# A fused attention and gated-GELU kernel on one core: the first stage put in another order (x ahead on two queues, exponentials grouped, M early, w_out clamped on VectorE)

## The chip, the cores and the metric

The kernel runs on one core of one Trainium2 chip. The metric is the device time of one execution in microseconds (us), as the median of several executions. All runs told here are in the same, fast state, and all of them gave correct results.

In views of the profile, PE is TensorE (matrix products), PEld its weight loads, DVE is VectorE, ACT is ScalarE, POOL is GpSimd, and SP the engine that issues most transfers. `L383` is line 383 of that kernel's own source, so the numbers of one statement differ between kernels.

## The reference, cut to what matters

```python
def _attn_ref(x, state):                       # x (8, 8, 512, 64), state (8, 8, 32, 64), fp32
    scores = scale * np.matmul(x, state.transpose(0, 1, 3, 2))
    a = softmax(scores)                        # (written out with max, exp and sum)
    xread = np.matmul(a, state)                # 512 tokens of a batch read the state
    scores2 = scale * np.matmul(state, x.transpose(0, 1, 3, 2))
    a2 = softmax(scores2)
    sread = np.matmul(a2, x)                   # 32 states of a batch read x
    return np.concatenate([xread, sread], axis=2)

def _moe_ref(x, w_in, w_out):                  # x (4352, 512), w_in (512, 2048), w_out (2048, 512)
    h = x @ w_in
    g = h * (1.0 / (1.0 + np.exp(-1.702 * h)))
    return (g @ w_out).astype(np.float32)
```

The weights arrive as 64-bit floating point. The kernel reads each number as two 32-bit words and puts a 32-bit number together from them with integer operations, on VectorE for the most part.

## The kernel before

Four ideas are needed for the argument.

**M.** `xread @ w_in` is computed as `a @ (state @ w_in)`. `M(b, c)` is the state of batch b times chunk c (512 columns) of w_in. An `up` tile then is four products of M with the softmax `aT`, followed by a gelu on ScalarE; `down` is the product with w_out. Batch b has 16 `up` tiles, four for each chunk; I call four of them a turn.

**Pieces.** w_in has 16 pieces of 128 x 512 numbers (piece 4c + k belongs to chunk c), w_out has 16 too. Each has two parts. `round_a` takes the exponent field and clamps it; `round_b` makes the number. Before, the clamp is two Relus on ScalarE for pieces 0 to 7 and two operations on POOL for all others.

```python
    def round_a(i):
        _, hi = words(i)
        sc = wpool.tile([P, FC], I32, tag="sc", name=f"sc_{i}", bufs=3)
        power[i] = sc
        nc.vector.tensor_scalar(sc, hi, 0x7FF00000, None, ALU.bitwise_and)
        if i >= 2 * NPR:
            nc.gpsimd.tensor_scalar(sc, sc, most, least, ALU.min, ALU.max)
            nc.gpsimd.tensor_scalar(sc, sc, -least, 8.0, ALU.add, ALU.mult)
            return
        nc.scalar.activation(out=sc.bitcast(FP32), in_=sc, func=AF.Relu, bias=edge[0], scale=-8.0)
        nc.scalar.activation(out=sc, in_=sc.bitcast(FP32), func=AF.Relu, bias=edge[1], scale=-1.0)

    def round_b(i):
        # ... cut: dst is the piece's place in w_in or w_out
        nc.vector.tensor_scalar(fr, hi, 0xFFFFF, 0x100000, ALU.bitwise_and, ALU.bitwise_or)
        nc.vector.scalar_tensor_tensor(sc, hi, -0x80000000, sc, ALU.bitwise_and, ALU.bitwise_or)
        nc.vector.scalar_tensor_tensor(dst, lo, 2.0**-32, fr, ALU.mult, ALU.add)
        nc.vector.scalar_tensor_tensor(dst, dst, 2.0**-20, sc.bitcast(FP32), ALU.mult, ALU.mult)

    AHEAD = 2                                   # exponents taken ahead of the piece that is rounded
```

**State reads.** Softmax over the tokens (exponentials on ScalarE, normalisation on VectorE), four transposes `eT` for each half, then 32 small products `sr`.

**Order.** Every engine takes its instructions in the order in which the program issues them. So where a statement stands in the program decides what waits behind what. This is the first stage of the kernel before:

```python
    load_weights(1)                             # piece 0, half a MB, ahead of x
    load_state(0)
    load_x(0)                                   # four chunks, all on SP's queue
    load_weights(NPR)
    # ...
    keep_warm(8)                                # products of zeros that keep TensorE's clock up
    round_to(1, 0)                              # piece 0
    att_state(0)
    att_xT(0, 0, 3)                             # three warm-up products before each x chunk
    # ... cut: scores and softmax of batch 0, piece 1, the same for batch 1, pieces 2 and 3

    def chunk(b, c, beside=()):
        round_to(NPR * (c + 1))
        att_M(b, c)
        for i in range(nper):
            up_x(b, nper * c + i)
            if i < len(beside):
                beside[i]()
    # ...
    chunk(0, 0, [lambda: None, lambda: att_x_exp(1), x_norm_1])
    chunk(1, 0, [rounds(1), rounds(1), rounds(1)])
    chunk(0, 1, [lambda: powers_to(done["b"] + 2), lambda: s_softmax(0), rounds(1), rounds(1)])
    chunk(1, 1, [rounds(1), rounds(1)])
    s_read(0)
    chunk(0, 2, [lambda: powers_to(done["b"] + 2), lambda: s_softmax(1), rounds(1), rounds(1)])
    s_read(1)
    chunk(0, 3, [rounds(1), rounds(1), rounds(1)])

    rest = list(range(2 * nper, NF))
    for f in range(NF):                         # the f loop: down of batch 0, rest of up of batch 1
        round_to(NFC * NPR + f + 1)
        for r in range(SCH):
            down(0, r, [f], out_x[0, r], r == SCH - 1)
        if f % 2:
            if rest[0] % nper == 0:
                att_M(1, rest[0] // nper)
            up_x(1, rest.pop(0))
        pace(1.5)
    # ... cut: batches 1 to 7
```

## Time and profile before

| kernel before | |
|---|---|
| median of the first 3 runs | 876.31 us (875.25 to 876.94) |
| span of the profiled run, mean granted clock | 874.7 us, 0.985 |
| PE busy | 851.0 us (97%) |
| f loop | 116.3 to 189.1 us |
| PE idle between 28.5 and 189.1 us | 15.1 us |

The profile page draws the span as 40 slices with one digit each (tenths of busy time). The other views used below are stretches (busy time of each engine between two times), the waits of an engine, and one engine's instructions in order of time. In that order a line has its start, its length, the engine and line, the operation, its tiles, and in brackets how long the engine had stood still before it and what ended that. The prediction below shows the main lines of before. Five more, in PE's order of time, are needed to weigh the result. The first is where the work that is compared later begins; the other four are the 20 us ahead of the f loop:

```profile
28.51 1.08 PE L251 MATMUL M<-w_in,stT 64*32 64x512 f32 x12
...
92.97 5.92 PE L334 MATMUL sr<-eT,xn 128*128 128x64 f32 x32 [1.48 <-ACT eT L327]
98.81 4.39 PE L251 MATMUL M<-w_in,stT 64*32 64x512 f32 x12
104.83 1.92 PE L251 MATMUL M<-w_in,stT 64*32 64x512 f32 x4 [1.63 <-DVE w_in L183]
107.42 9.07 PE L375 MATMUL h<-aT,M 128*128 128x512 f32 x16 [0.67 <-ACT M L317]
```

The groups of the last four lines take elsewhere in this trace 3.79 (the state read at 76.22), 1.08 (twelve products of M at 52.16), 1.05 (the last four at 29.87) and 7.13 us (a turn at 82.45). So the loss of these 20 us is not in brackets alone: TensorE also works slowly, because its clock is halved after the waits and because M(0,3) gets its pieces one by one.

### The profile page before, as it was taken

The page shows a single profiled execution, that of the slowest core. Times are in us where ns is not written, and L with a number is a line of the kernel's source. Part 1 is how long each engine was busy: PE and PEld are TensorE (multiplying, and loading weights), DVE is VectorE, ACT ScalarE, POOL GpSimd, SP SyncE. Part 2 cuts the span into 40 slices and gives each one's busy share as a digit, 9 for nine tenths or more (in the row PEclk, how much of TensorE's full clock was granted, in tenths as well). Part 3 has the DMA queues.
Part 4 walks back from the last instruction along what each step waited for, and adds up shares of the span by engine and source line. Part 5 has one row for each costly group of instructions (what it writes and reads, how often), then busy time and mean ns, then how long its engine had stood idle before and what let it go on. Part 6 is the DMA issues. An engine that isn't in the chain of part 4 may idle for free.

```text
span 874.7 us, 6893 instructions
## 1 busy us (share of the span) xinstructions
PE 851.0 (97%) x2892; PEld 394.0 (45%) x2892; DVE 222.9 (25%) x370; ACT 199.9 (23%) x335; POOL 59.2 (7%) x90
## 2 busy tenths in 40 slices
PE   8889799999999999999999999999999999999997
PEld 3324444444354435444454435443544447744443
DVE  5856999203300050005000230005000500000000
ACT  4653310112123120412122212312041212103100
POOL 0012444010000000000000000000000000000000
PEclk9999699999999999999999999999999999999999
DMA  9602045310020001200030003000000000000000
GB/s 242 244 1 96 7 153 163 69 52 12 25 61 0 16 13 29 44 3 25 12 61 4 12 21 64 1 12 13 13 12 1 24 13 13 1 12 12 13 12 24
DMA packets 43134, 35.04 MB, mean 40 GB/s; under 512 B 36832, under 2 KB 36832, under 8 KB 43104
## 3 DMA queue, kind: packets, MB, share of 16 engines
q1 hardware_dynamic: 40000, 25.69, 10.8%
q0 software_dynamic: 3104, 8.92, 2.8%
q8 instruction: 22, 0.36, 0.2%
q14 instruction: 8, 0.07, 0.0%
HBM read 25.69 MB, written 8.91 MB: 40 GB/s over the span
## 4 chain that ended last, share of the span: by engine, by line
issue 71%; PE 19%; DVE 5%; ACT 2%; POOL 2%; DMA 1%; SPq 0%; POOLq 0%; DVEq 0%; ACTq 0%
PE o L400 11%; PE h L375 5%; POOL out_dram L408 2%; PE M L251 1%; DVE w_in L182 1%; DVE sc L181 1%; DVE w_in L183 1%; DMA xn<-in_x_dram 1%; ACT g L377 0%; ACT M L317 0%; PE sr L334 0%; PE xT L243 0%; DVE sc L165 0%; PE s L251 0%; DVE fr L180 0%
## 5 line engine op out<-in xcount | busy, mean ns | idle before, releaser
L400 PE MATMUL o<-w_out,g 128*128 128x512 f32 x1024 | 456.3, 595 | 0.0
L400 PEld LDWEIGHTS o<-w_out,g 128*128 128x128 f32 x1024 | 188.8, 190 | 232.3 <-issue 231.3
L375 PE MATMUL h<-aT,M 128*128 128x512 f32 x512 | 231.0, 607 | 9.5 <-ACT M L317 6.1
L375 PEld LDWEIGHTS h<-aT,M 128*128 128x128 f32 x512 | 98.0, 194 | 142.1 <-issue 115.0
L377 ACT ACTIVATE g<-h 128x512 f32<-128x512 f32 x128 | 76.1, 597 | 169.7 <-PE h L375 169.6
L317 DVE COPY M<-M 128x512 f32<-128x512 f32 x24 | 16.4, 682 | 194.6 <-PE M L251 194.6
L408 POOL DMA_DIRECT2D out_dram<-osb x32 | 17.5, 548 | 644.7 <-ACT osb L407 644.5
L407 ACT COPY osb<-o 128x512 f32<-128x512 f32 x32 | 18.7, 585 | 136.1 <-PE o L400 133.8
L251 PE MATMUL M<-w_in,stT 64*32 64x512 f32 x512 | 43.9, 615 | 2.7 <-DVE w_in L183 2.7
L317 ACT COPY M<-M 128x512 f32<-128x512 f32 x40 | 22.6, 587 | 83.9 <-PE M L251 83.9
L334 PEld LDWEIGHTS sr<-eT,xn 128*128 128x128 f32 x256 | 31.8, 203 | 5.6 <-issue 2.9
L334 PE MATMUL sr<-eT,xn 128*128 128x64 f32 x256 | 31.8, 286 | 2.3 <-ACT eT L327 2.3
L234 DVE COPY stT<-stT 128x128 f32<-128x128 f32 x6 | 1.7, 290 | 117.2 <-PE stT L232 117.2
L244 ACT COPY xT<-xT 128x512 f32<-128x512 f32 x18 | 10.3, 586 | 91.0 <-PE xT L243 91.0
L375 PE MATMUL h_sr<-srT,w_in 128*128 128x256 f32 x128 | 27.8, 379 | 0.0
L400 PE MATMUL o_sr<-w_out,g 128*128 128x512 f32 x64 | 27.6, 592 | 0.0
L244 DVE COPY xT<-xT 128x512 f32<-128x512 f32 x14 | 9.7, 692 | 65.5 <-PE xT L243 65.5
L375 PEld LDWEIGHTS h_sr<-srT,w_in 128*128 128x128 f32 x128 | 24.3, 190 | 3.7 <-issue 0.5
L167 POOL TENSOR_SCALAR sc<-sc 128x512 int32<-128x512 int32 x24 | 17.3, 722 | 110.4 <-DVE sc L165 110.4
L243 PEld LDWEIGHTS xT<-ident,xn 128*128 128x128 f32 x128 | 15.7, 141 | 16.9 <-issue 12.7
L264 DVE STREAM_TRANSPOSE e<-s 128x512 f32<-128x512 f32 x16 | 10.5, 694 | 47.1 <-PE s L251 47.1
L343 DVE COPY srT<-sr 64x128 f32<-64x128 f32 x6 | 1.7, 283 | 81.4 <-PE sr L334 81.4
(64 smaller groups left out, 393.1 us busy)
## 6 DMA issues: line engine op xcount, KB each, us to landing
xn<-in_x_dram SPq DMA_DIRECT2D x32, 256.0 KB
raw_o<-in_moe_w_out_dram SPq DMA_DIRECT2D x16, 512.0 KB
out_dram<-osb POOLq DMA_DIRECT2D x32, 256.0 KB, 2.3
w_out<-in_moe_w_in_dram SPq DMA_DIRECT2D x12, 512.0 KB
raw_i<-in_moe_w_in_dram SPq DMA_DIRECT2D x4, 512.0 KB
stn<-in_state_dram SPq DMA_DIRECT2D x16, 32.0 KB
out_dram<-osb_sr POOLq DMA_DIRECT2D x2, 256.0 KB, 7.1
```

The source lines that it names most:

```text
L167: nc.gpsimd.tensor_scalar(sc, sc, most, least, ALU.min, ALU.max)
L243: nc.tensor.transpose(ps[:, c], x_heads(b, c, j), ident)
L244: copies(b or None, j)(A[b]["xT"][:, j], ps.rearrange("p c q -> p (c q)"))
L251: nc.tensor.matmul(ps[g][st], A[b]["stT"][rows, st], rhs(rows, j), start=True, stop=True)
L264: nc.vector.transpose(t[:, g].rearrange("p i n -> p (i n)"), a["s"][g])
L317: copies(b, g)(m[:, g], ps[g])
L334: nc.tensor.matmul(ps[:, j], x_heads(b, c, j), a["eT"][:, :, c, Ns * j : Ns * (j + 1)], start=(c == 0), stop=(c == SCH - 1),)
L375: nc.tensor.matmul(hps, lhs[i], rhs[i], start=(i == 0), stop=(i == n - 1))
L377: nc.scalar.activation(out=gt[:, :ntok], in_=hps, func=AF.Gelu_apprx_sigmoid)
L400: nc.tensor.matmul(ops, G[key, f][:, P * r : P * (r + 1)], w_out[:, f], start=(f == 0), stop=(f == NF - 1))
L407: nc.scalar.copy(osb, ops)
L408: nc.gpsimd.dma_start(dst, osb)
```

## The change

Its intent is to close the holes of the first stage. x is to come before the weights, on two queues. The exponentials of both batches' state reads are to share one swap of ScalarE's function table instead of two. `M` is to be computed ahead of its turn where that is possible. The clamp of w_in goes wholly to ScalarE and that of w_out to VectorE, so that POOL no longer works beside VectorE. Exponents are taken three pieces ahead, but only within w_in. The state reads move into the f loop, spread out. (Left out of the diff: the fraction of a piece, `fr`, is made in place instead of in a tile of its own, and the function for the state reads' softmax is cut into maximum, exponential and normalisation.)

```diff
@@ load_x
-            nc.sync.dma_start(xn[b][:, c], x_v[b, c])
+            queue = nc.scalar if b == 0 and c % 2 else nc.sync
+            queue.dma_start(xn[b][:, c], x_v[b, c])
@@ round_a                                     (AHEAD is 3 now; sc has AHEAD + 1 buffers)
-        if i >= 2 * NPR:
-            nc.gpsimd.tensor_scalar(sc, sc, most, least, ALU.min, ALU.max)
-            nc.gpsimd.tensor_scalar(sc, sc, -least, 8.0, ALU.add, ALU.mult)
+        if PIECES[i][0] == "o":
+            nc.vector.tensor_scalar(sc, sc, most, least, ALU.min, ALU.max)
+            nc.vector.tensor_scalar(sc, sc, -least, 8.0, ALU.add, ALU.mult)
             return
@@ round_to
-            powers_to(done["b"] + 1 + ahead)
+            powers_to(min(done["b"] + 1 + ahead, max(NFC * NPR, done["b"] + 1)))
@@ the first stage (cut: two and 24 warm-up products instead of three and 18, order of the head)
-    load_weights(1)
     load_state(0)
     load_x(0)
...
-    round_to(1, 0)
     att_state(0)
-    att_xT(0, 0, 3)
+    att_xT(0, 0, 2)
...
+    att_blocks(1)
+    att_x_exp(1)
+    up_x(0, 0)
+    up_x(0, 1)
+    up_x(0, 2, True)                            # True: a PSUM tile of another pool
+    up_x(0, 3, True)
+    round_to(NPR + 1)
+    att_x_norm(1)
+    att_M(1, 0)
+    # turn(b, c, then, n): the four up of a turn, M of "then" before the last, n pieces beside
+    turn(1, 0, None, [1, 1])
+    round_to(2 * NPR)
+    att_M(0, 1)
+    turn(0, 1, (1, 1), [1, 1, 1])
+    turn(1, 1, None, [1])
+    round_to(3 * NPR)
+    att_M(0, 2)
+    att_s_max(0)
+    att_s_max(1)
+    turn(0, 2, None, [1, 1, 1])
+    room = apool.tile([P, NPR, S], FP32, tag="xT", name="e2_0")
+    att_s_exp(0, room)
+    att_s_exp(1)
+    round_to(4 * NPR)
+    att_M(0, 3)
+    att_s_norm(0)
+    att_s_norm(1)
+    turn(0, 3, None, [1, 1])
@@ the f loop
     for f in range(NF):
+        rounds(1)
         round_to(NFC * NPR + f + 1)
         for r in range(SCH):
             down(0, r, [f], out_x[0, r], r == SCH - 1)
-        if f % 2:
-            if rest[0] % nper == 0:
-                att_M(1, rest[0] // nper)
+        if f in (0, nper * 2):
+            att_M(1, 2 + f // (nper * 2))
+        if f in (0, 2):
+            for g in range(NG):
+                att_eT(f // 2, g)
+        if f in (1, 3):
+            att_sread(f // 2)
+        if f % 2 == 1:
             up_x(1, rest.pop(0))
-        pace(1.5)
```

More of the change, by code (lines that the diff above doesn't have):

```diff
@@ L127 @@
     raw, power = {}, {}
+    AHEAD = 3
     def load_weight(i):
@@ L162, in round_a @@
         _, hi = words(i)
-        sc = wpool.tile([P, FC], I32, tag="sc", name=f"sc_{i}", bufs=3)
+        sc = wpool.tile([P, FC], I32, tag="sc", name=f"sc_{i}", bufs=AHEAD + 1)
         power[i] = sc
         nc.vector.tensor_scalar(sc, hi, 0x7FF00000, None, ALU.bitwise_and)
-        if i >= 2 * NPR:
-            nc.gpsimd.tensor_scalar(sc, sc, most, least, ALU.min, ALU.max)
-            nc.gpsimd.tensor_scalar(sc, sc, -least, 8.0, ALU.add, ALU.mult)
+        if PIECES[i][0] == "o":
+            nc.vector.tensor_scalar(sc, sc, most, least, ALU.min, ALU.max)
+            nc.vector.tensor_scalar(sc, sc, -least, 8.0, ALU.add, ALU.mult)
             return
@@ L175, in round_b @@
         dst = w_in[key[1]][:, key[2]] if key[0] == "i" else w_out[:, key[1]]
+        fr = dst.bitcast(I32)
         lo, hi = words(i)
         sc = power.pop(i)
-        fr = wpool.tile([P, FC], I32, tag="fr", name=f"fr_{i}")
         nc.vector.tensor_scalar(fr, hi, 0xFFFFF, 0x100000, ALU.bitwise_and, ALU.bitwise_or)
@@ L184, in round_b @@
         del raw[i]
-    AHEAD = 2
     done = {"load": 0, "a": 0, "b": 0, "credit": 0.0}
@@ L264, in att_blocks, with att_s_max, att_s_exp @@
             nc.vector.transpose(t[:, g].rearrange("p i n -> p (i n)"), a["s"][g])
-    def att_s_exp(b):
+    def att_s_max(b):
+        a = A[b]
+        a["mx2"] = []
+        for g in range(NG):
+            mx = apool.tile([P, 1], FP32, tag="mx2", name=f"mx2_{b}_{g}", bufs=4)
+            nc.vector.tensor_reduce(out=mx, in_=a["s"][g], axis=AX.X, op=ALU.max, negate=True)
+            nc.vector.tensor_scalar(mx, mx, scale, None, ALU.mult)
+            a["mx2"].append(mx)
+    def att_s_exp(b, room=None):
         a = A[b]
@@ L269, in att_s_exp, with att_s_norm @@
         for g in range(NG):
-            mx = apool.tile([P, 1], FP32, tag="mx2", name=f"mx2_{b}_{g}", bufs=2)
-            nc.vector.tensor_reduce(out=mx, in_=a["s"][g], axis=AX.X, op=ALU.max, negate=True)
-            nc.vector.tensor_scalar(mx, mx, scale, None, ALU.mult)
-            e = apool.tile([P, S], FP32, tag="e2", name=f"e2_{b}_{g}", bufs=2)
-            sm = apool.tile([P, 1], FP32, tag="sm2", name=f"sm2_{b}_{g}", bufs=2)
-            nc.scalar.activation(out=e, in_=a["s"][g], func=AF.Exp, bias=mx, scale=scale, accum_out=sm)
+            e = apool.tile([P, S], FP32, tag="e2", name=f"e2_{b}_{g}", bufs=2) if room is None else room[:, g]
+            sm = apool.tile([P, 1], FP32, tag="sm2", name=f"sm2_{b}_{g}", bufs=4)
+            nc.scalar.activation(out=e, in_=a["s"][g], func=AF.Exp, bias=a["mx2"][g], scale=scale, accum_out=sm)
             a["e2"].append((e, sm))
-    def att_s_softmax(b):
+    def att_s_norm(b):
         for e, sm in A[b]["e2"]:
@@ L356, in att_slots @@
         at(5, att_blocks, b)
+        at(5, att_s_max, b)
         at(5, att_s_exp, b)
         at(5, att_x_exp, b)
-        at(5, att_s_softmax, b)
+        at(5, att_s_norm, b)
         at(5, att_x_norm, b)
@@ L369, with up @@
     G = {}
-    def up(key, f, ntok, lhs, rhs):
-        hps = psH.tile([P, ntok], FP32, tag="h", name=f"h_{key}_{f}")
+    def up(key, f, ntok, lhs, rhs, spare=False):
+        hps = att_ps([P, ntok], f"h_{key}_{f}") if spare else psH.tile([P, ntok], FP32, tag="h", name=f"h_{key}_{f}")
         n = len(lhs)
@@ L378, in up, with up_x @@
         G[key, f] = gt
-    def up_x(b, f):
+    def up_x(b, f, spare=False):
         c, o = divmod(P * f, FC)
         m = A[b]["M", c]
-        up(b, f, S, [m[:, g, o : o + P] for g in range(NG)], [A[b]["aT"][:, g] for g in range(NG)])
+        up(b, f, S, [m[:, g, o : o + P] for g in range(NG)], [A[b]["aT"][:, g] for g in range(NG)], spare)
     def up_s(f):
@@ L408, in down, with rounds @@
             nc.gpsimd.dma_start(dst, osb)
-    load_weights(1)
+    nper = FC // P
+    def rounds(n):
+        round_to(done["b"] + n)
     load_state(0)
@@ L425 @@
     att_scores(0)
-    powers_to(2)
+    powers_to(1)
     att_blocks(0)
     att_x_exp(0)
+    powers_to(2)
     round_to(2, 1)
     att_x_norm(0)
-    keep_warm(18)
+    keep_warm(24)
     att_state(1)
@@ L436, with turn @@
     att_scores(1)
-    keep_warm(18)
-    round_to(NPR, 1)
-    nper = FC // P
-    def chunk(b, c, beside=()):
-        round_to(NPR * (c + 1))
-        att_M(b, c)
+    keep_warm(24)
+    powers_to(4)
+    round_to(NPR, 2)
+    att_M(0, 0)
+    att_blocks(1)
[7 more added lines that the diff above has]
+    att_M(1, 0)
+    def turn(b, c, then, n=()):
         for i in range(nper):
+            if i == nper - 1 and then:
+                att_M(*then)
             up_x(b, nper * c + i)
-            if i < len(beside):
-                beside[i]()
-    powers_to(NPR + 1)
-    att_blocks(1)
-    def x_norm_1():
-        round_to(NPR + 1, 1)
-        att_x_norm(1)
-    def s_softmax(b):
-        att_s_exp(b)
-        att_s_softmax(b)
-    def s_read(b):
-        for g in range(NG):
-            att_eT(b, g)
-        att_sread(b)
-    def rounds(n):
-        return lambda: round_to(done["b"] + n)
-    chunk(0, 0, [lambda: None, lambda: att_x_exp(1), x_norm_1])
-    chunk(1, 0, [rounds(1), rounds(1), rounds(1)])
-    chunk(0, 1, [lambda: powers_to(done["b"] + 2), lambda: s_softmax(0), rounds(1), rounds(1)])
-    chunk(1, 1, [rounds(1), rounds(1)])
-    s_read(0)
-    chunk(0, 2, [lambda: powers_to(done["b"] + 2), lambda: s_softmax(1), rounds(1), rounds(1)])
-    s_read(1)
-    chunk(0, 3, [rounds(1), rounds(1), rounds(1)])
+            if i < len(n):
+                rounds(n[i])
+    turn(1, 0, None, [1, 1])
[16 more added lines that the diff above has]
+    turn(0, 3, None, [1, 1])
     rest = list(range(2 * nper, NF))
     for f in range(NF):
+        rounds(1)
         round_to(NFC * NPR + f + 1)
@@ L484 @@
             down(0, r, [f], out_x[0, r], r == SCH - 1)
-        if f % 2:
-            if rest[0] % nper == 0:
-                att_M(1, rest[0] // nper)
+        if f in (0, nper * 2):
+            att_M(1, 2 + f // (nper * 2))
+        if f in (0, 2):
+            for g in range(NG):
+                att_eT(f // 2, g)
+        if f in (1, 3):
+            att_sread(f // 2)
+        if f % 2 == 1:
             up_x(1, rest.pop(0))
-        pace(1.5)
     load_state(2)
```

## The prediction

> **What bounds the kernel now.** I read three views in this order: the 40 slices of the page, the busy time by stretch, and the chain of waits with the order of time of each engine.
>
> ```profile
> PE   8889799999999999999999999999999999999997
> DVE  5856999203300050005000230005000500000000
> PEclk9999699999999999999999999999999999999999
> ```
>
> TensorE (PE) is full from the seventh slice on; the loss is in the first six, where VectorE (DVE) is the busier of the helpers, and one slice has a low clock. The stretches put numbers on it:
>
> ```profile
> 28.50:116.30 87.80, 74.18 (x273) 32.99 (x273) 65.84 (x110) 39.87 (x66) 21.57 (x27) 0.86 0.20 72
> 116.30:189.10 72.80, 71.29 (x194) 30.62 (x193) 41.92 (x61) 8.69 (x15) 19.17 (x24) 1.00 0.39 108
> 189.10:874.70 685.60, 680.09 (x2295) 319.09 (x2293) 96.00 (x168) 138.63 (x234) 17.71 (x32) 1.00 0.07 19
> ```
>
> Columns: stretch, length, then busy time of PE, weight load, DVE, ACT, POOL, then granted clock. From 189.1 us (the `down` of batch 1) PE is busy 680 of 686 us, and the change touches nothing there. So the question is only when that point is reached. The useful PE work between 28.5 and 189.1 us at full clock is: 32 `up` tiles at 1.72 us (55.0), 64 `down` products at 0.859 (55.0), 8 `M` blocks at 1.05 (8.4), two eT at 0.88 (1.8), two state reads at 3.5 (7.0; both as the later batches show them): 127 us of 160.6. About 33 us are lost, nearly all before 116 us.
>
> The chain of waits shows how, in the third turn:
>
> ```profile
> 60.07 1.28 ACT L275
> 61.36 1.45 ACT e L275 x4
> 62.83 1.28 ACT L377
> 64.12 1.09 ACT g L377 x2
> 65.21 0.49 ACT M L317
> 65.74 8.85 PE h L375 x16
> ```
>
> ScalarE (ACT) swaps its function table for two exponentials and back, so the gelus and the copy of `M` queue up behind it and PE starts at 65.74 although `M` was ready at 63.87. The sum of the waits has the other side: DVE stood still for those exponentials, twice, while weight pieces were still to be rounded.
>
> ```profile
> DVE sm L281 <- ACT e L275: 16.1, 2, 9.4
> ```
>
> Those 16 us come back at 90 to 105 us, where PE waits for the last four pieces of w_in. Two more lines, from DVE's order of time, show what a piece costs alone and beside POOL:
>
> ```profile
> 27.81 0.69 DVE L181 SCALAR_TENSOR_TENSOR sc<-w_out,sc 128x512 int32<-128x512 int32 x1
> 64.42 1.10 DVE L181 SCALAR_TENSOR_TENSOR sc<-raw_i,sc 128x512 int32<-128x512 int32 x1
> ```
>
> From start to start a piece takes 2.60 us with POOL quiet (27.14 to 29.74) and 3.54 with POOL clamping (63.75 to 67.29). Last, the clock after an idle stretch of PE (39.75 to 42.83):
>
> ```profile
> 42.00:43.00 1.00, 0.17 (x1) 0.20 (x2) 1.00 (x3) 1.00 (x3) 0.00 (x0) 1.00 0.00 0
> 43.00:44.00 1.00, 1.00 (x2) 0.44 (x2) 1.00 (x3) 0.01 (x1) 0.00 (x0) 0.54 0.00 0
> 46.00:47.00 1.00, 1.00 (x3) 0.53 (x2) 0.39 (x2) 0.61 (x2) 0.77 (x2) 0.75 0.00 0
> ```
>
> It is halved for 3.4 us (43.05 to 46.5), which costs 1.7; again 3.4 us from 66.9, and 17 us from 94.3.
>
> **What the Trainium skill says.** (1) "TensorE: Matmul & The Clock Gate", section "What's actually happening": the clock is halved after an idle window of 3413 ns; the windows run free. The trace agrees: 43.05, 66.94, 94.3 and 111.3 lie on one grid of 3.413 us. Windows with about 45% of PE work or less were punished, one with about 60% was not (53.3 to 56.7). (2) "ScalarE: Activation LUTs", "What ACT_TABLE_LOAD costs": 1283 ns plus a drain of about 1380 for each switch. The load agrees (1.28); the drain doesn't show: the exponential starts at 61.36, 1.29 after the load began. I use 1.3 a switch. (3) "GPSIMD Engine Reference", "8. Key points": POOL shares its SBUF interfaces with DVE, with contention for instructions of two SBUF inputs. It agrees: 0.69 against 1.10 above. (4) "VectorE: DVE Perf Modes", "The perf-mode tier table": tensor_scalar in fp32 runs at 2x from SBUF. In this trace the int32 bit operation of a piece (0.34 from start to start) is about twice as fast as the two-input ones (0.60 to 0.70). Whether min/max and add/mult on int32 do so is not shown; I assume 0.37 each.
>
> **The change part by part.** I walk the four in-order queues of the changed build with the durations above (gelu 0.60, ACT's two Relus 1.37 a piece, copy of `M` to first `up` 0.64, result of a matmul 0.26 after its issue, exponential of 512 columns 0.72).
>
> x ahead: before, the four chunks of x land at 6.5, 7.7, 8.9, 9.95, behind 0.5 MB of weights. Without these, and issued from two queues, I take the last at 7.7 (an estimate: the same 1.2 us a chunk from 2.3, plus landing). The scores of batch 0 end at 11.75 instead of 13.94: 2.2 gained.
>
> The head of DVE: piece 0 was rounded in DVE's idle time while x came; now it comes after the scores. From 11.75: blocks, maximum, subtraction 3.75, then pieces 0 and 1 (2.60 each), norm 4.27, pieces 2 and 3 with two more exponents taken ahead (5.54): 30.5, against 29.87. So the 2.2 are spent and 0.6 more; the first `up` starts at 32.2 (31.59 before).
>
> Batch 1 exponentials ahead of the gelus: one table swap before the four `up` of batch 0, which spare PSUM lets run through (to 39.1). Then the trap: in ACT's order the exponents of pieces 6 and 7 (2 x 1.37) stand ahead of the copy of `M` (1,0). Last gelu 40.0, exponents to 42.75, `up` (1,0) at 43.4; before 42.83. PE idles 0.9 + 2.3 us here.
>
> w_in clamped on ACT instead of POOL for pieces 8 to 15: 0.94 us less on DVE for each, 7.5 in all, for 1.37 each on an ACT that is at 45%. Pieces 4 to 7 are ready at 49.3 (before 54.0), PE gets to `M` (0,1) at 50.3; its copy waits behind one exponent, `up` (0,4) at 53.1 (before 55.72). `M` (1,1) ahead of its turn: its copy runs under `up` (0,7), gap 0.55 instead of 1.87+; `up` (1,4) at 61.6 (before 65.74), `M` (0,2) at 68.4, `up` (0,8) at 70.15 (before 82.45, with one state read done), to 77.0. Pieces 8 to 11 are ready at 59.7, 12 to 15 at 76.1: no wait.
>
> The grouped exponentials: table, 4 x 0.72, and only then the copy of `M` (0,3), done on PE at 78.05: 82.05, `up` (0,12) at 82.7 (before 107.42, with both state reads done). PE idles 4.65 us here, the largest hole that is left. Saved: four of seven table loads, 5.1 us of ACT, and the 16 us of DVE's waits.
>
> From 82.7: four `up`, 6.9, so the f loop starts at 89.6 (before 116.3). It is longer than before: 64 `down` 55.0, 8 `up` 13.8, two `M` 2.1, and now both eT 1.8 and both state reads 7.0, waits 0.7: 80.4, end 170.0. DVE needs 3.35 for a w_out piece (2.60 and two clamps), the loop 4.3 at least, so PE stays the bound, and the state reads now lie between dense products.
>
> The clock: holes of 0.9 + 2.3 (39 to 43), 1.8 (51 to 53) and 4.65 (78 to 83). With the rule of about half a window, and the phase of the windows unknown, I expect 1.4, 0.75 (a chance of 45% of 1.7) and 1.7: 3.85 together. End of the f loop 173.8, before 189.1: 15.3 gained. From there nothing differs: 876.3 - 15.3 = 861.0 us.
>
> **The rivals.** First, the clock: the holes could each be punished fully (1.7, 1.7, 2.6), or phases be kind (0, 0, 0.9). For it speaks that before lost its clock in each comparable hole; the ends are 863 and 858. Second, x does not come earlier: DMA already moves 220 to 280 GB/s there and x has rows of 256 bytes, so a second queue may add only contention, and piece 0 must still be rounded on the way. Then all shifts by 1.5 to 2: 863. Against it: half a MB of weights no longer stands ahead of x. Third, DVE becomes the bound in the f loop: if the clamps on int32 run at 0.6 to 1.0 each, a piece takes 3.8 to 4.6 against PE's 4.3, with two pieces of lead at the start; at the worst 2 to 4 us are lost at its end: 864. Fourth, the whole gain of 33 us: if the ACT queue did not block `M`, the f loop would end at about 160 and the time be 848; the order on ACT, fixed by the program, speaks against it.
>
> **Range and chances.** 861.0, spread about 3 us from the clock (2), the arrival of x (1) and small waits that a walk leaves out (1.5, mostly upward, against which the kinder clock stands). Range 857.0 to 865.5. Over 2% faster needs under 858.8, 0.7 of the spread below the middle: 0.27. Slower by 2% would need all of the gain and 17 us more to be lost: 0.01.
>
> **What would show it right or wrong.** Last x chunk near 7.7 and scores ended near 11.75; pieces 2.6 us apart with no POOL work after 2 us; the `M` (1,0) copy behind two exponents, near 42.8; one table load for four exponentials near 78 and a hole of 4 to 5 us with a half clock after it; the f loop from 89.6 to 92 up to 170 to 176 without a DVE wait, w_out pieces near 3.35. It is wrong if PE waits for DVE in the f loop, if the state reads there pull the clock down, or if the time after the f loop differs from 685.6.

## The result, and the profile after

| | before | after |
|---|---|---|
| median of 4 runs | 875.78 us | 863.03 us |
| lowest to highest | 874.36 to 876.94 | 860.92 to 863.76 |
| profiled run | 876.46 us | 862.39 us |
| mean granted clock of the profiled run | 0.985 | 0.996 |
| f loop | 116.3 to 189.1 us | 94.2 to 175.0 us |

All outputs are right. Ratios here are the mean time of one kernel's runs over the mean of the other's of the same rounds, so they are not quite the ratios of the medians quoted. The ratio after to before is 0.9851 (95% interval 0.9827 to 0.9876): 1.5% less time.

The page's slices of the changed kernel:

```profile
PE   8987999999999999999999999999999999999997
DVE  4996996005000320005000510014000500000000
PEclk9999999999999999999999999999999999999999
```

The low slice of the clock (the fifth of before) is gone. Apart from the first, PE's weakest slices are now the third and fourth, where the holes shown below lie. DVE stands at 9 in the second and third slices, where it had 8 and 5. The stretches, with the columns as in the prediction:

```profile
29.00:94.20 65.20, 55.51 (x208) 21.07 (x207) 56.74 (x112) 43.46 (x73) 0.00 (x0) 0.97 0.24 83
94.20:175.00 80.80, 80.07 (x274) 39.38 (x273) 47.06 (x96) 11.88 (x23) 1.22 (x2) 1.00 0.36 104
175.00:860.60 685.60, 680.12 (x2295) 319.11 (x2293) 96.05 (x168) 138.78 (x234) 17.79 (x32) 1.00 0.07 19
```

The last stretch is as long as before, to the second decimal: 685.60 us. All of the gain is in the first two, which end 14.1 us earlier (189.1 against 175.0); the profiled runs differ by 14.07 (876.46 against 862.39). For a comparison of equal work, the count has to start at the first product of M(0,0): at 28.51 before, at 32.13 after. (The first stretch of after begins at 29.0 and holds 15 warm-up products too.) From there to the end of the f loop TensorE does the same 466 products. They took 160.6 us before, 145.5 busy and 15.1 idle, and 142.9 us after, 132.5 busy and 10.4 idle. So the change gained 17.7 us here, 4.7 of idle and 13.0 of busy time, and lost 3.6 in the head, by which M(0,0) starts later; 14.1 are left.

The groups of before that took longer than the same groups elsewhere account for most of the 13.0: a half-clocked part of a turn at 42.83 (7.08 us for twelve products, 5.42 at full clock), the turn at 65.74 (8.83 against 7.13), and the last four lines shown before. That is 1.66 + 1.70 + 2.13 + 3.31 + 0.87 + 1.94 = 11.6 us. After has one such group, 8.83 instead of 7.13; the difference is 9.9. Of the other 3.1, about 2.1 are M blocks: two more of them than after ran in two steps, as their pieces came one by one, which takes 2.13 us instead of 1.09. So nearly three quarters of what was gained behind the head were not idle time by name: they were slow work, nearly all of it after or between waits.

VectorE's waits for the state reads' exponentials, as the view of the waits has them:

```profile
DVE sm L288 <- ACT e L282: 3.8, 1, 3.8
```

They were 16.1 us in two waits before. PE's order of time in the head of the changed kernel:

```profile
7.71 0.47 PE L244 MATMUL xT<-ident,xn 128*128 128x128 f32 x1 [0.75 <-DMA xn<-in_x_dram]
7.98 1.06 PE L103 MATMUL warm<-g 128*128 128x512 bf16 x2
8.83 0.42 PE L244 MATMUL xT<-ident,xn 128*128 128x128 f32 x1
...
12.89 1.80 PE L252 MATMUL s<-xT,stT 64*32 64x512 f32 x16
...
32.13 1.08 PE L252 MATMUL M<-w_in,stT 64*32 64x512 f32 x12
33.62 1.05 PE L252 MATMUL M<-w_in,stT 64*32 64x512 f32 x4 [0.41 <-DVE w_in L185]
```

The first chunk of x is there at 7.71, where before the four were taken up at 6.56, 7.77, 8.95 and 9.98. Then each chunk costs about 1.1 us of PE (two warm-up products and a transpose) until 10.8, and the scores end at 14.7. Before, they ended at 13.9. The last step of M(0,0) is at 33.62, against 29.87 before.

The chain also ran at half clock. Two warm-up products took 0.85 us from start to start (7.98 to 8.83), and 0.43 later in this trace (23 of them from 14.84 to 19.81). The view of the stretches doesn't show it: the trace's first record of the clock, full speed, lies at 10.64 us, and before its first record that view prints 1.00.

The same view further on shows the three holes that are left in front of a turn, and the start of the f loop:

```profile
46.36 7.13 PE L383 MATMUL h<-aT,M 128*128 128x512 f32 x16 [2.12 <-ACT M L324]
...
56.02 5.42 PE L383 MATMUL h<-aT,M 128*128 128x512 f32 x12 [1.51 <-ACT M L324]
...
85.52 8.83 PE L383 MATMUL h<-aT,M 128*128 128x512 f32 x16 [4.23 <-ACT M L324]
94.19 3.60 PE L408 MATMUL o<-w_out,g 128*128 128x512 f32 x8
```

Each waits for ScalarE's copy of `M`. What ScalarE does before the third one, in its own order of time:

```profile
80.91 1.28 ACT L282 ACT_TABLE_LOAD   x1
...
84.87 1.08 ACT L324 COPY M<-M 128x512 f32<-128x512 f32 x2
85.97 1.28 ACT L385 ACT_TABLE_LOAD   x1
```

Between the two lies nothing but the four exponentials. The turn behind the hole took 8.83 instead of 7.13 us: the clock was at 0.50 from 85.7 to 89.1, one window. Between the head and the last 3.5 us of the span, where TensorE has no more work, it was low nowhere else in this run.

### The profile page after: what moved, and what is told of

Same layout as the page of the kernel before. It is cut to its first block, busy times and chain, and to the rows that moved or that the text cites. A ratio compares the mean times of both kernels' runs of the same rounds, so it can differ in the third digit from the quotient of the medians.

```text
span 860.6 us, 6881 instructions
## 1 busy us (share of the span) xinstructions
PE 841.0 (98%) x2898; PEld 391.0 (45%) x2900; DVE 215.9 (25%) x402; ACT 205.5 (24%) x347; POOL 19.8 (2%) x42
## 4 chain that ended last, share of the span: by engine, by line
issue 72%; PE 21%; DVE 2%; POOL 2%; ACT 2%; DMA 1%; SPq 0%; POOLq 0%; ACTq 0%
PE o L408 11%; PE h L383 7%; POOL out_dram L416 2%; PE M L252 1%; PE sr L341 1%; DMA xn<-in_x_dram 1%; PE xT L244 0%; ACT M L324 0%; PE s L252 0%; ACT e L282 0%; DVE w_in L185 0%; DVE w_in L184 0%; DVE sc L183 0%; PE warm L103 0%; ACT sc L173 0%
## 5 line engine op out<-in xcount | busy, mean ns | idle before, releaser
L383 PE MATMUL h<-aT,M 128*128 128x512 f32 x512 | 227.2, 599 | 9.3 <-ACT M L324 9.3
L415 ACT COPY osb<-o 128x512 f32<-128x512 f32 x32 | 18.8, 586 | 136.3 <-PE o L408 134.0
L252 PE MATMUL M<-w_in,stT 64*32 64x512 f32 x512 | 37.8, 601 | 0.4 <-DVE w_in L185 0.4
L341 PEld LDWEIGHTS sr<-eT,xn 128*128 128x128 f32 x256 | 29.8, 192 | 3.8 <-issue 3.8
L341 PE MATMUL sr<-eT,xn 128*128 128x64 f32 x256 | 29.4, 273 | 0.0
L103 PE MATMUL warm<-g 128*128 128x512 bf16 x74 | 20.9, 431 | 1.5 <-DVE one L97 1.2
```

Source lines behind the costliest of these rows:

```text
L103: nc.tensor.matmul(ps, zeros[:, :P], zeros, start=True, stop=True)
L252: nc.tensor.matmul(ps[g][st], A[b]["stT"][rows, st], rhs(rows, j), start=True, stop=True)
L341: nc.tensor.matmul(ps[:, j], x_heads(b, c, j), a["eT"][:, :, c, Ns * j : Ns * (j + 1)], start=(c == 0), stop=(c == SCH - 1),)
L383: nc.tensor.matmul(hps, lhs[i], rhs[i], start=(i == 0), stop=(i == n - 1))
L415: nc.scalar.copy(osb, ops)
```

## The experiments

The result asks two questions. The first: what part of the change brought the 14 us, and did some parts bring nothing? The second: the head came out 3 us later than predicted; why? For the second there were two readings. One puts the loss on PE: x is all there at 7.7 us, and the chain of warm-up products and transposes that follows is what takes long. The other puts it on the transfers: with two queues the first chunk lands later, the last no sooner than before, and the chain, which had been hidden between the arrivals, runs at the end. (The letters A and B in the expectations below are each run's own.)

Twelve kernels were run, each in four executions, in three batches. The kernel before ran beside them: 876.18, 875.75 and 875.33 us (medians). All edits are against the changed kernel. A caution for all of them: the changed kernel's own four runs span 2.8 us, with mean clocks of 0.998, 0.996 and twice 0.994 for 860.92, 862.39, 863.76 and 863.68 us. One window of 3.4 us at half clock is worth 1.7 us, which is 0.002 of the span, so these runs differ by one or two windows. Differences under 2 us are therefore read from the traces rather than from the medians.

### The head: x on one queue

```diff
-            queue = nc.scalar if b == 0 and c % 2 else nc.sync
+            queue = nc.sync
```

> The changed kernel with all four chunks of x on the one queue again, still ahead of the weights. Theory A (two queues make x complete sooner, and that sets the scores): last chunk at 8.5 us or later, scores of batch 0 end 0.5 to 1 us later than 14.7, total 863 to 865. Theory B (two queues make all chunks land together, so the chain of transposes and warm-up products, one chunk after another, starts at 7.7 us instead of with the first chunk): first transpose at about 5.5 us, transposes overlap with the arrival, scores end at 12.5 to 13.5, total 1.2 to 2.2 us lower than the changed kernel, 861 to 862.

Measured: 862.41 us (860.65 to 862.96), ratio to before 0.9845 (0.9821 to 0.987). PE's order of time of this kernel:

```profile
5.46 0.33 PE L244 MATMUL xT<-ident,xn 128*128 128x128 f32 x1
...
8.96 0.76 PE L244 MATMUL xT<-ident,xn 128*128 128x128 f32 x5 [0.33 <-DMA xn<-in_x_dram]
...
44.54 8.83 PE L383 MATMUL h<-aT,M 128*128 128x512 f32 x16 [2.12 <-ACT M L324]
```

With one queue the chunks can be used one after the other (transposes at 5.46, 6.67, 7.87 and 8.96), and the scores end at 12.9, which is 1.8 us earlier than with two. The last step of M(0,0) is 1.8 earlier too (31.80). So theory B of this run holds: the second queue delayed the first transpose by 2.2 us, and it brought nothing that a single queue doesn't bring: there all four chunks are in use by 8.96.

The clock takes part in the 1.8 us. Here full clock is recorded from 4.76 us on; in all eight traces with two queues and warm-up products the chain from 7.7 to 10 us ran at half clock, and their scores end between 14.7 and 15.5. At full clock a chunk of batch 1 takes 0.76 us with three warm-up products (20.56 to 21.32 in the changed kernel), so some 0.54 with two. By this estimate the three steps from 7.71 to 10.81, 3.1 us, would have been 1.6: about 1.5 us are the clock's. No run separates it from the late arrival, which left PE idle before.

The total doesn't show the lead: in the profiled run the clock fell at 45.7, in the turn that begins at 44.54 (8.83 instead of 7.13), and again from 83.3 to 90.1. By 94.67, where its f loop begins, the lead was gone.

### The head: no warm-up products at x

```diff
-    att_xT(0, 0, 2)
+    att_xT(0, 0)
```

> The changed kernel with two queues, without the two warm-up products ahead of each transpose of the first x. Theory B: the four transposes run back to back at about 7.7 to 8.5 us, scores end at about 12.5 (14.7 with them), total 2 us lower, about 861. Theory A (the chunks themselves arrive one after another up to 10.8): scores end unchanged at 14.5 or so, total unchanged at 863. A lower clock in the first 30 us would show that the warm-up products were needed.

Measured: 863.81 us (862.00 to 864.61), ratio 0.9862 (0.9836 to 0.9887). The scores end at 13.85, 0.9 earlier than in the changed kernel; M(0,0) ends 0.8 earlier. The third transpose still waited 0.55 us for its data, until 8.85, and the fourth followed without a wait, so the last chunk of x is there at about 8.9. Without warm-up products the clock was recorded at 0.50 from 8.5 to 12.0 us, so what the chain lost in length it partly lost again in speed, and another window at half clock from about 46.0 to 49.5 took the rest. So neither theory of this expectation holds as it stands. The warm-up products cost 0.9 us and not 2.2, and x was complete neither at 7.7, as I had also predicted, nor at 10.8, but at about 8.9, on two queues as on one.

### The head: undone in part

```diff
+    load_weights(1)                             # piece 0 first again; x on one queue as above
...
+    round_to(1, 0)
     att_state(0)
-    att_xT(0, 0, 2)
+    att_xT(0, 0, 3)
```

> The changed kernel with the old head: first weight piece ahead of x, one queue, piece 0 rounded while x arrives. My theory says that the new head is a loss by itself, as it moves 2.6 us of rounding into DVE's unbroken chain and the scores don't end earlier: scores end at 13.9, the last M(0,0) step starts at 30 (33.6 in the changed kernel), total 3 to 3.7 us lower, about 859.5. The rival (the new head helps, as intended): total 865 or more.

Measured: 862.97 us (861.59 to 863.41), ratio 0.9852 (0.9824 to 0.9881). The expectation was missed, and the trace says why: the undoing was incomplete. The scores end at 14.1, but the 24 warm-up products of the changed kernel (18 before) hold PE until 31.2, and VectorE waited 1.48 us for the exponent of piece 1, which the changed order takes later. So M(0,0) ran in one go at 31.28, and the first `up` began at 34.03.

### The head: undone wholly

```diff
 (the edits of the run above, and)
-    powers_to(1)
+    powers_to(2)
...
-    keep_warm(24)
+    keep_warm(18)                               # both places
```

> The changed kernel with the old head in full: first weight piece ahead of x, one queue, piece 0 rounded while x arrives, the exponent of piece 1 before the scores, 18 warm-up products instead of 24. In the earlier undoing the 24 warm-up products held PE up to 31.2 and DVE waited 1.5 us for the exponent of piece 1. Theory (new head is a loss by itself): last M(0,0) step starts at 30.0 to 30.3 (33.6 in the changed kernel), everything up to the f loop comes 3.3 to 3.6 us earlier, total 859 to 860. Rival: a clock window or another wait gives it back, total 862 or more.

Measured: 859.89 us (859.35 to 861.14), ratio 0.9825 (0.9797 to 0.9853). The last step of M(0,0) is at 30.43, and the f loop begins at 90.99 instead of 94.19. So the new head by itself is a loss of about 3 us; the rest of the change is worth about 3 us more than the whole. Most of this is not the arrival of x: the scores end at 14.2, only 0.5 earlier than in the changed kernel. The rest is piece 0, 2.60 us of VectorE, which here is rounded while x comes.

### The third hole: M(0,3) copied before the exponentials

```diff
-    att_s_exp(0, room)
-    att_s_exp(1)
     round_to(4 * NPR)
     att_M(0, 3)
+    att_s_exp(0, room)
+    att_s_exp(1)
     att_s_norm(0)
     att_s_norm(1)
-    turn(0, 3, None, [1, 1])
+    for i in range(nper):
+        up_x(0, 3 * nper + i, i >= 2)           # the last two on PSUM tiles of another pool
+        if i < 2:
+            rounds(1)
```

> The changed kernel with the copy of M(0,3) ahead of the four grouped exponentials on ACT, and the last two up tiles of that turn in spare PSUM. Theory: the hole of 4.2 us before up(0,12) is the ACT queue, and the half clock after it is its result: the hole falls to 0.7 us, no low clock after it, f loop starts 5 to 5.7 us sooner, total 857 to 858. Rival: PE then waits for the gelus or DVE's normalisation instead, and the gain is under 2 us.

Measured: 860.67 us (859.90 to 863.58), ratio 0.9835 (0.9806 to 0.9864). PE's order of time:

```profile
84.21 7.13 PE L383 MATMUL h<-aT,M 128*128 128x512 f32 x16 [0.75 <-ACT M L324]
93.61 5.37 PE L408 MATMUL o<-w_out,g 128*128 128x512 f32 x8 [2.27 <-issue]
```

and VectorE's:

```profile
86.77 0.15 DVE L288 TENSOR_SCALAR sm<-sm 128x1 f32<-128x1 f32 x1 [5.43 <-ACT e L282]
```

The hole shrank from 4.23 to 0.75 as intended, but another took part of its place: PE stood for 2.27 us before the first `down`. The trace calls it issue; VectorE shows what it was. Its normalisations stood in its queue ahead of the first w_out piece and waited 5.43 us for the exponentials, so this piece was ready at 93.5 only. The first eight `down` then took 5.37 instead of 3.60 at half clock. (The turn starts only 1.3 us earlier than in the changed kernel because this run's first `up` came 0.7 later, at 36.02, and a window of low clock from 46.7 cost it 1.5.)

### The third hole, with the normalisation after the first w_out pieces

```diff
 (the edit of the run above, and)
-    att_s_norm(0)
-    att_s_norm(1)
     for i in range(nper):
         up_x(0, 3 * nper + i, i >= 2)
         if i < 2:
             rounds(1)
+    att_s_norm(0)
+    att_s_norm(1)
```

> As the run with the copy of M(0,3) ahead of the exponentials, where the hole closed but PE then waited 2.3 us for the first w_out piece, as DVE's normalisation waited for the later exponentials and stood ahead of that piece. Here the normalisation comes after two w_out pieces. Theory (the hole is only a matter of the order on ACT and DVE): both waits gone, f loop starts at about 89 (94.2 in the changed kernel), total 857 to 858.5. Rival: something else takes their place (PE waits for eT or spare PSUM), total 860 or more.

Measured: 857.39 us (857.17 to 859.72), ratio 0.9800 (0.9771 to 0.9830). PE's order of time:

```profile
82.01 7.13 PE L383 MATMUL h<-aT,M 128*128 128x512 f32 x16 [0.76 <-ACT M L324]
88.98 3.60 PE L408 MATMUL o<-w_out,g 128*128 128x512 f32 x8
```

Both waits are gone, no low clock follows (mean 0.999), and the f loop starts 5.2 us earlier than in the changed kernel: 3.5 of the hole and 1.7 of its window. The hole was a matter of the order on ScalarE, as the prediction said, and what took its place was a matter of the order on VectorE.

### The first two holes: M copied before the exponents

```diff
-    round_to(NPR + 1)
+    round_to(NPR + 1, 1)
     att_x_norm(1)
     att_M(1, 0)
+    powers_to(2 * NPR)
...
-    round_to(2 * NPR)
+    round_to(2 * NPR, 2)
     att_M(0, 1)
+    powers_to(2 * NPR + 3)
```

> The changed kernel with the copies of M(1,0) and M(0,1) ahead of the exponents of the next pieces on ACT, nothing else. Theory: the waits of PE before up(1,0) and up(0,4), 2.12 and 1.51 us, fall to about 0.7 each; the later exponents still come in time for DVE; total 2.2 us lower, about 861. Rival: DVE waits for the later exponents and M(0,1) starts later, total unchanged.

Measured: 861.38 us (859.84 to 862.00), ratio 0.9834 (0.9810 to 0.9859). The waits before `up` (1,0) and (0,4) fell from 2.12 to 0.71 and from 1.51 to 0.75, 2.2 us together, as expected. But `up` (0,4) begins at 54.56 instead of 56.02, only 1.5 earlier: the first `up` came 0.3 later in this run, and the turn of `up` (1,0) took 0.4 longer (7.55 instead of 7.13). In the profiled run the third hole then cost more (two windows at half clock, and a turn of 9.92 instead of 8.83 us), so the f loop started only 0.4 us earlier, at 93.81.

### The state reads in a row

```diff
+    for b in (0, 1):                            # ahead of the f loop
+        for g in range(NG):
+            att_eT(b, g)
+        att_sread(b)
...
-        if f in (0, 2):
-            for g in range(NG):
-                att_eT(f // 2, g)
-        if f in (1, 3):
-            att_sread(f // 2)
```

> The changed kernel with both state reads one after the other just ahead of the f loop, instead of between its dense products. Theory (spreading them keeps the clock up): the waits for the eT copies come bare, 1.5 us more, and the two reads of 3.5 us with 64 columns each lose at least one clock window, total 866 to 869. Rival (a read at full pace keeps the clock as well as a dense product, and the old loss came from the waits around it): total 864.5 to 865.

Measured: 864.85 us (863.98 to 866.30), ratio 0.9878 (0.9854 to 0.9903). The reads took 3.79 us each, as at full clock, so small products in a row do not pull the clock down here. They waited for ScalarE's copies of `eT` (0.78 and 0.68 us) and of `srT` (0.18), waits that dense products cover in the changed kernel. Spreading the reads is worth 1.5 us by the traces (both f loops' work begins at 94.2 and ends at 176.49 here, at 174.99 in the changed kernel).

### The clamp of w_in on POOL again (pieces 8 to 15)

```diff
         nc.vector.tensor_scalar(sc, hi, 0x7FF00000, None, ALU.bitwise_and)
+        if 2 * NPR <= i < NFC * NPR:
+            nc.gpsimd.tensor_scalar(sc, sc, most, least, ALU.min, ALU.max)
+            nc.gpsimd.tensor_scalar(sc, sc, -least, 8.0, ALU.add, ALU.mult)
+            return
```

> The changed kernel with the clamp of w_in pieces 8 to 15 on POOL again, as before the change, instead of on ACT. Theory of the prediction (0.94 us less on DVE for each of eight pieces is worth something): the last piece of w_in is ready 4 to 8 us later than 79, PE waits for it, total 866 to 869. Rival (in the new order DVE has slack there, as the grouped exponentials hold PE until 85.5 anyway, and ACT is rid of 1.37 us a piece): last piece at 83 to 85, the wait of 1.5 us before up(0,4) shrinks, total 861.5 to 863.5.

Measured: 863.63 us (863.21 to 864.33), ratio 0.9867 (0.9844 to 0.9890). The last quarter of M(0,3) waited 0.37 us for its piece, and ScalarE, free of those Relus, copied M(0,1) sooner (the wait before `up` (0,4) is 0.76 instead of 1.51). In the new order VectorE has slack in this stage, so the 7.5 us of its time that the prediction counted for moving this clamp were real but off the path: they bought nothing that the runs can tell. If anything they cost a little: from the first `up` to the f loop this run takes 59.7 us, 1.6 of them for a low window at 47 that the changed kernel didn't meet, and the changed kernel takes 58.9.

### The clamp of w_out on POOL again

```diff
         if PIECES[i][0] == "o":
-            nc.vector.tensor_scalar(sc, sc, most, least, ALU.min, ALU.max)
-            nc.vector.tensor_scalar(sc, sc, -least, 8.0, ALU.add, ALU.mult)
+            nc.gpsimd.tensor_scalar(sc, sc, most, least, ALU.min, ALU.max)
+            nc.gpsimd.tensor_scalar(sc, sc, -least, 8.0, ALU.add, ALU.mult)
...
-            powers_to(min(done["b"] + 1 + ahead, max(NFC * NPR, done["b"] + 1)))
+            powers_to(done["b"] + 1 + ahead)
```

> The changed kernel with the clamp of the w_out pieces on POOL, and exponents ahead, as before the change. Theory: a piece costs DVE 3.53 us with its own clamps in the changed trace and cost 3.54 beside POOL before, so nothing changes and DVE isn't the bound in the f loop: total 862 to 864. Rival (POOL's share of the memory port slows the normalisation or the copies): over 865.

Measured: 871.93 us (869.35 to 872.42), ratio 0.9955 (0.9929 to 0.9982). The expectation was missed by 8 us. VectorE's order of time:

```profile
94.70 0.43 DVE L167 TENSOR_SCALAR sc<-raw_o 128x512 int32<-128x512 int32 x1 [2.68 <-DMA raw_o<-in_moe_w_out_dram]
...
101.00 0.43 DVE L167 TENSOR_SCALAR sc<-raw_o 128x512 int32<-128x512 int32 x1 [2.78 <-DMA raw_o<-in_moe_w_out_dram]
```

A w_out piece takes some 6.2 us here (88.51, 94.70, 101.00, 107.16), and 2.6 to 2.8 of them are waits for a transfer. There are four buffers for raw pieces. With exponents three ahead, VectorE takes the exponent of the piece three further on before it rounds this one, and that piece's buffer was freed only by the piece just done. So the time of a load lies in every piece. From 142 us on PE waited for VectorE (0.76 to 2.47 us, at five places). The f loop takes 88.5 us instead of 80.8. The run changed two things at once, the engine of the clamp and the cap on exponents ahead, and it is not the kernel before in this respect: there two exponents were ahead, not three, and a w_out piece took 3.55 us without such a wait. The waits for transfers point to the cap; what POOL alone would cost was not run and stays open. (One figure of it shows: beside POOL the two-input operations take 1.10 and 1.09 us instead of 0.68, as they did before.)

### The exponentials not grouped

```diff
+    # in turn(): after the second up, if "soft" names a batch
+                att_s_max(soft)
+                att_s_exp(soft, room if soft == 0 else None)
+                att_s_norm(soft)
...
-    turn(0, 1, (1, 1), [1, 1, 1])
+    turn(0, 1, (1, 1), [1, 1, 1], 0)
...
-    att_s_max(0)
-    att_s_max(1)
-    turn(0, 2, None, [1, 1, 1])
-    att_s_exp(0, room)
-    att_s_exp(1)
+    turn(0, 2, None, [1, 1, 1], 1)
     round_to(4 * NPR)
     att_M(0, 3)
-    att_s_norm(0)
-    att_s_norm(1)
```

> The changed kernel with the exponentials not grouped: each batch has its own maximum, two exponentials and normalisation in the middle of a turn of batch 0, as before the change. Theory (grouping saves two table loads of 1.28 us and DVE's waits, but makes one hole of 4.2 us and mostly one clock window): the hole at 81 to 85 goes, DVE stands still 5 to 7 us twice again, two shorter holes of 2 to 4 us appear, total within 2 of 863. Rival (grouping was the gain): 868 or more.

Measured: 876.25 us (873.96 to 878.37), ratio 1.001 (0.998 to 1.0039). All that the change had gained is gone; my expectation was missed and the rival was right. VectorE's waits in this run:

```profile
DVE sm L288 <- ACT e L282: 18.9, 2, 11.5
```

and PE's order of time:

```profile
72.18 9.84 PE L383 MATMUL h<-aT,M 128*128 128x512 f32 x16 [5.54 <-ACT M L324]
...
94.36 1.59 PE L252 MATMUL M<-w_in,stT 64*32 64x512 f32 x4 [2.45 <-DVE w_in L185]
...
101.48 8.85 PE L383 MATMUL h<-aT,M 128*128 128x512 f32 x16 [0.67 <-ACT M L324]
```

The pattern of before is back. VectorE has done the maxima and has only the normalisation next, so it stands for 7.4 and 11.5 us until ScalarE, behind its gelus and a table load, has made the exponentials. Meanwhile ScalarE in turn waits 1.4 us for VectorE's next exponent, with the copy of M(1,1) queued behind it, and PE waits 5.54 us for that copy. The pieces of chunk 3 are late by 2.45 us and more. Two stretches of low clock follow (from 70.8 and from 94.7 us), and the f loop starts at 110.2 instead of 94.2. (2.3 of these 16 us are not the exponentials: this run's first `up` came 0.6 later, and a low window at 47 cost 1.7.) Grouping the exponentials, with the maxima ahead and the normalisation behind other work, is worth about 13 us in this order: as much as the whole gain, in which the head's loss and some smaller gains about cancel.

### The best parts together

The old head with 18 warm-up products, M copied before the exponents and before the exponentials, and the late normalisation: the edits above together, on the grouped order of the changed kernel.

> All that helped together: the changed kernel with the old head and 18 warm-up products, the copies of M(1,0), M(0,1) and M(0,3) ahead of exponents and exponentials, normalisation after two w_out pieces. If the parts add up (3.4 + 2.2 + 5.2 from the changed kernel's 863.0): 852 to 853, 0.973 of the kernel before. If one wait takes another's place, 855 to 857.

Measured: 852.81 us (852.68 to 853.09), ratio to before 0.9743 (0.9718 to 0.9769): clearly faster than before. PE's order of time:

```profile
77.56 7.13 PE L383 MATMUL h<-aT,M 128*128 128x512 f32 x16 [0.75 <-ACT M L324]
84.53 3.60 PE L408 MATMUL o<-w_out,g 128*128 128x512 f32 x8
```

The f loop starts 9.7 us earlier than in the changed kernel. That is about what the three parts gave, each read from the start of its f loop or of the turn that it touched: 3.2 for the head, 1.5 for the first two holes and 5.2 for the third, 9.9 in all. All four runs had a mean clock of 0.999, and they lie within 0.4 us of each other, against 2.8 in the changed kernel: where no hole of some microseconds is left, there is no window for the clock to fall in, and the scatter goes too.

## Why the prediction was right, and where it was off

The prediction of 861.0 us, between 857.0 and 865.5, and most likely within 2%, held: 863.03. The 1.2 us by which the end of the f loop was off in the profiled run (175.0 against 173.8) is a sum of larger terms of both signs.

**x ahead (2.2 us gained by the scores).** This step was wrong in size and in sign. I took the last chunk at 7.7 us and the scores' end at 11.75. But 7.7 is when the first chunk arrived, the last came at about 8.9, and the scores ended at 14.7: 3.0 us later, and 0.8 later than before. The second rival, that a second queue adds no sooner arrival, was right in kind. What I had left out is the serial chain that the arrivals had been hiding: warm-up products and a transpose for each chunk, 1.1 us from one to the next, and at half clock: by the estimate above about 1.5 of the 3.0 us. With one queue, still ahead of the weights, 1.8 of the 3.0 came back, so even then the scores ended 1.2 later than predicted. The old head wins its 3 us in another way, as told above.

**The head of DVE (18.75 us from the scores to the last piece).** Right: 14.7 to 33.5, or 18.8. So the 3 us went through unchanged to the first `up`, at 35.33 instead of 32.2.

**The copy of M(1,0) behind two exponents; `up` (0,4) behind one.** Right in kind and size: waits of 2.12 and 1.51 us where I had 2.3 and 1.8, and ScalarE's order as written. The run with M before the exponents showed the cause.

**w_in clamped on ScalarE (7.5 us of DVE).** VectorE saved it, but the run with POOL back shows that it was off the path. The walk came out right in spite of this, because I had read its gain off where PE's waits end, not off the sum.

**The grouped exponentials.** Right: one table load at 80.91, four exponentials, the copy of M(0,3), and a hole of 4.23 us where I had 4.65. Ungrouping them took 13 us back. What the prediction named first among the savings, four table loads (two of which come from the grouping, 2.6 us of ScalarE), is the smaller part. The stall of VectorE behind the exponentials, which it counted as 16 us, is the larger; 3.8 of it remained.

**The f loop (80.4 us).** Right: 80.8, with no wait for VectorE. A w_out piece took 3.53 us where I had assumed 3.35, since clamps that depend on the operation before them start 0.46 us apart rather than 0.37. Each lasts 0.43 us, like the bit operation and unlike the 0.68 of operations with two tensor inputs, so what was assumed of int32 came out nearly right. The third rival, VectorE as the bound there, did not come true: four `down` and the rest leave more time than that. The state reads did not pull the clock down.

**The clock (3.85 us lost in three holes).** Too pessimistic, and this hid the first error: in the profiled run only the largest hole was punished, with 1.7 us. That is 2.15 less than I counted. 3.1 us for the head, 2.15 less for the clock and 0.4 more in the f loop make 1.35; the 4.23 instead of 4.65 in the third hole brings that down to 0.9, so 0.3 of the measured 1.2 stay with small waits. That the total came within 2.1 us of 861.0 is thus in part luck: two errors of 3.1 and 2.15 us had opposite signs.

That the holes cost a window or two more or less by chance fits the spread of the runs, 860.92 to 863.76 at clocks of 0.998 to 0.994; only one of these runs has a trace, so this was read from the mean clocks and not seen.

Which of the holes between 1 and 3 us are punished can be read from the traces, with the grid of 3.413 us laid from a recorded change of the clock. The hole of 2.12 us before `up` (1,0) lay across a boundary of the grid in the changed kernel (44.77; the window up to 48.18 was 53% busy, and not punished), and inside one window in the one-queue run (42.31 to 45.72, 38% busy, punished). In the fourteen traces each window at full clock with 45% or less was followed by half clock, and none with 59% or more. Between 48% and 57% both happened: 49% and 57% were punished, 48%, 51% and 53% were not. The 57% is a window of the kernel before, 90.87 to 94.28, ahead of its longest low stretch, which the prediction's rule left out.

**The fourth rival, the whole gain of 33 us.** Rightly ruled out: ScalarE's order still held `M` back. But it was not a fixed bound. Three changes of order freed 9.7 us more.

Some points stay open. What the clamp of w_out on POOL costs with no exponents ahead was not run. Nor was M(1,1) ahead of its turn undone alone (the trace shows its wait of 1.87 us gone), nor the early exponentials of batch 1 with their spare PSUM tiles. And the runs do not show where between 48% and 57% the clock's threshold lies, or what else it counts.

## What to carry to other kernels

Where engines work in program order, a group of instructions that waits for another engine should stand behind everything that doesn't need it. Here splitting maximum, exponential and normalisation, and putting other work between them, was worth 13 us, while moving 7.5 us of VectorE's work to another engine was worth nothing that the runs could tell. Before transfers are spread over two queues, look at what their staggered arrival hides: if the first lands later and the last no sooner, work that had been hidden comes to light. And a hole of a few microseconds costs more than its length when the clock falls behind it, so read the length of the groups after it against the same group elsewhere in the trace.

## What the Trainium skill lacked or had wrong

- "TensorE: Matmul & The Clock Gate", section "What's actually happening": the free-running windows agree (before's low clocks begin at 43.08, 66.97 and 94.28, and the last ends at 111.35, all on one grid of 3.413 us). What it lacks is how much work a window needs to escape: here all windows at full clock with 45% of PE busy or less were punished, none with 59% or more, and between 48% and 57% some. It also has no figure for what such windows do to whole runs of one kernel: the same kernel ran in 860.92, 862.39 and 863.76 us at mean clocks of 0.998, 0.996 and 0.994.
- "ScalarE: Activation LUTs", section "What ACT_TABLE_LOAD costs": 1.28 us for the load agrees. The drain of about 1.38 us that it adds to each switch did not show: the last gelu ended and the load began at 80.91, and the first exponential at 82.20.
- "DMA: Bandwidth & Descriptors", section "Issuing engines are not separate DMA queues": it agrees that a second issuing engine adds no bandwidth (x was complete at about 8.9 us on two queues as on one). It lacks the price of it: with interleaving, the first of four 256 KB chunks landed at 7.7 us instead of before 5.5.
- "GPSIMD Engine Reference", section "8. Key points": the contention with VectorE agrees, and it can be given a size: 1.10 us instead of 0.68 for an operation with two inputs while POOL worked.
